# Loading the first input pair in two-chunk transfers, in an FFT-then-SoLU kernel on Trainium2

## The chip, the cores and the metric

The kernel runs on one core of one Trainium2 chip. The metric is device time in microseconds (us) of one execution; below 0.2% (2.4 us) a difference can't be told from no change. Engines are called PE (TensorE, matmul), DVE (VectorE), ACT (ScalarE), POOL (GpSimd) and SP (SyncE, which only issues transfers here). POOL issues the indirect (gathering) transfers; these go through another queue (q0) than SP's (q1).

## What is computed

```python
# x: (8, 3136, 256) float32; w_in (256, 1024), w_out (1024, 256), g_ln (1024): float64
X = np.fft.fft(np.fft.fft(x, axis=1), axis=2).real      # (8, 3136, 256)
x = X.reshape(25088, 256)
h = x @ w_in
e = np.exp(h - h.max(-1, keepdims=True))
solu = h * e / (e.sum(-1, keepdims=True) + 1e-09)
ln = (solu - mean(solu)) / np.sqrt(var(solu) + 1e-06) * g_ln
out = ln @ w_out                                        # (25088, 256) float32
```

## The kernel before

The sequence length 3136 is split as 49 x 64 (`N1`, `N2`), and the batch of 8 into four pairs (`Pair`). One pair gives 98 partitions (`PR`: two batch entries by 49 rows n1); row n1 of an entry is 64 positions of 256 floats, so neighbouring partitions lie 64 KB apart in DRAM. Because the input is real, position n2 is folded with its mirror position: only 32 of 64 positions (`NH`) are transformed. They are worked in eight **chunks** (`NC`) of four positions (`CH`); a chunk is 4 KB in each partition, 392 KB in all.

For each chunk `load` (L107) issues two transfers: SP fetches `xa` (L115), POOL gathers the mirrored rows `xb` through an index table (L117). The last chunk also fetches `x0` (L123). `add_mirror` (L132) adds the two on DVE, `fold` (L140) folds the features into `y` on DVE, `transform1` (L151) multiplies `y` with the table `F` on PE (L182), ACT copies the result to a tile `z` (L185), and `keep` (L189) writes 20 or, for later pairs, all of its 100 rows to a DRAM buffer `zd`. When all eight chunks are in `zd`, `turn` (L192) reads it back turned round, and `transform2` (L200) makes the input of a unit of 128 tokens. The hundred units (four pairs by 25) then run through a software pipeline: `up` (L233, two products with `Wi`), `even`, `join`, exponent, product, square, transposition and `down` (products with `Wo`).

The first pair has nothing to hide behind, and its load shares the start with the weights. These are float64 and are turned to float32 on the chip: four pieces of `w_in` are loaded (`piece_in`, L480) into `raw_in`; each goes through `exponent_in` (DVE L483, three ACT instructions L505 to L507) and `narrow_in` (DVE L483, L519, L522, L527); `product_in` (L577) multiplies them with the DFT table `Q`. `w_out` is loaded to `raw_out` by `load_out` (L589) and narrowed after the last chunk.

The order on every engine is the order of the program text (`tc.manual_schedule()`). In the start this is, on SP: index table, pieces 0 and 1, x of chunk 0, `F`, piece 2, chunk 1, piece 3, chunks 2 and 3, `Q`, `g_ln`, chunks 4 and 5; then, between the chunks' work, chunk 6 (after the fold of chunk 0), the `zd` write of chunk 0, chunk 7 (after the fold of chunk 1) and so on. Chunks 2 to 5 go into spare tiles that the main loop needs later (the `uT` buffers, "rooms" of four 4 KB rows each: `xa` and `xb` of two chunks), the others into the two buffers of `xpool`. On DVE, the program order is: exponents 0 and 1, narrowing 0 and 1, exponent 2, chunk 0, narrowing 2, exponent 3, chunk 1, narrowing 3, chunks 2 to 7, exponents of `w_out`. `load_out` stands after the fold of chunk 3 in the text and so behind the `zd` write of chunk 2 on SP; `product_in(0)` follows the transform of chunk 3 on PE, `product_in(1)` and `(2)` that of chunk 7.

A transfer on SP has one of eight completion semaphores in turn, and waits until the transfer eight places before it has landed. A transfer of 98 partitions runs on 14 of the 16 DMA engines, seven rows on each: of the 16 counts of its semaphore, 14 come as its engines end, spread over some microseconds.

Of the kernel before, what the change touches and what calls it, by code (L numbers as in the profile page):

```python
# [9 lines left out]
FP32 = mybir.dt.float32  # L10
# [7 lines left out]
P = 128  # L18
# [5 lines left out]
PR = 2 * N1  # L24
ZR = 4 * NK
CH = 4
NC = NH // CH

KG = 5
# [6 lines left out]
def kernel(  # L36
# [19 lines left out]
    nc = tc.nc  # L56
    B, S, D = x.shape
    FF = moe_w_in.shape[1]
    KF = FF // P
# [5 lines left out]
    x_pn = x.rearrange("b (n1 n2) d -> (b n1) n2 d", n2=N2)  # L65
# [10 lines left out]
    fpool = ctx.enter_context(tc.tile_pool(name="fpool", bufs=2))  # L76
# [3 lines left out]
    F = const.tile([PR, 6, ZR], FP32, name="F")  # L80
# [4 lines left out]
    Ws = const.tile([P, 4, KF // 2, P], FP32, name="Ws")  # L85
# [9 lines left out]
    def result(i):  # L95

        return ps_m.tile([P, 2 * D], FP32, tag=f"m{i % 4}", name="ps_m")

    class Pair:
        def __init__(self, p):
            self.p = p
            self.raw, self.y, self.y0 = {}, {}, None
            self.g, self.zs, self.done = {}, {}, []

    def load(pr, c, room=None):  # L107

        r = slice(pr.p * PR, (pr.p + 1) * PR)
        if room is None:  # L110
            xa = xpool.tile([PR, CH, D], FP32, tag="xa", name="xa")
            xb = xpool.tile([PR, CH, D], FP32, tag="xb", name="xb")
        else:
            xa, xb = (t.rearrange("p (l d) -> p l d", d=D) for t in room)
        nc.sync.dma_start(out=xa, in_=x_pn[r, c * CH + 1 : (c + 1) * CH + 1, :])  # L115
        i = pr.p * NC + c
        nc.gpsimd.indirect_dma_start(  # L117
            out=xb.rearrange("p l d -> p (l d)"), out_offset=None, in_=x_g,
            in_offset=bass.IndirectOffsetOnAxis(ap=idx[0:PR, i : i + 1], axis=0))
        x0 = None  # L120
        if c == NC - 1:
            x0 = xpool.tile([PR, 1, D], FP32, tag="x0", name="x0", bufs=1)
            nc.sync.dma_start(out=x0, in_=x_pn[r, 0:1, :])  # L123
        pr.raw[c] = (xa, xb, x0)
# [7 lines left out]
    def add_mirror(pr, c, engine):  # L132

        xa, xb, _ = pr.raw[c]
        n = CH - 1 if c == NC - 1 else CH
        a, rb = xa[:, 0:n, :], xb[:, ::-1, :][:, 0:n, :]
        engine.tensor_tensor(out=a[:, :, 1:D], in0=a[:, :, 1:D], in1=rb[:, :, D - 1 : 0 : -1], op=ALU.add)
        engine.tensor_tensor(out=a[:, :, 0:1], in0=a[:, :, 0:1], in1=rb[:, :, 0:1], op=ALU.add)

    def fold(pr, c):  # L140

        xa, _, x0 = pr.raw.pop(c)
        y = xpool.tile([PR, CH, D], FP32, tag="y", name="y")
        copy = nc.scalar.copy if pr.p else nc.vector.tensor_copy
        fold_features(y, xa, copy)
        pr.y[c] = y
        if c == NC - 1:
            pr.y0 = xpool.tile([PR, 1, D], FP32, tag="y0", name="y0", bufs=1)
            fold_features(pr.y0, x0, copy)

    def transform1(pr, s):  # L151

        c, l = divmod(2 * s, CH)
        if s == 0:
            pr.zd = dram.tile([ZR, NH, D], FP32, tag="zd", name="zd")
        if l == 0:

            if pr.p or c < 2:  # L160
                pr.z = zpool.tile([ZR, CH, D], FP32, tag="z", name="z")
            elif c < 4:
                z = fpool.tile([P, FF], FP32, tag="u", name="z_u", bufs=2)
                pr.z = z[0:ZR].rearrange("p (l d) -> p l d", l=CH)
            elif c < 6:
                pr.z = Ws.rearrange("p (h w) c k -> h p (w c k)", h=2)[c - 4, 0:ZR].rearrange("p (l d) -> p l d", l=CH)
            elif c == 6:
                pr.z = spool.tile([ZR, CH, D], FP32, tag="z6", name="z6")
            else:
                pr.z = gpool.tile([P, KG, D], FP32, tag="g", name="z_g")[0:ZR, 0:CH, :]  # L170
            pr.zs[c] = pr.z
        y = pr.y[c]
        ps = result(0 if pr.p else s).rearrange("p (l d) -> p l d", l=2)
        if s == NH // 2 - 1:
            parts = [(ps[0:ZR, 0], y[:, l], 0), (ps[0:ZR, 1], pr.y0[:, 0], 1), (ps[0:ZR, 1], y[:, l + 1], 2)]
        else:
            parts = [(ps[0:ZR], y[:, l : l + 2], 0)]
        pr.done.append(s)
        first = True
        for o, i, t in parts:  # L180
            for h, cs in enumerate((EVEN, ODD)):
                nc.tensor.matmul(o[..., cs], F[:, 2 * t + h, :], i[..., cs], start=first, stop=True,  # L182
                                 skip_group_check=True)
                first = False
        nc.scalar.copy(pr.z[:, l : l + 2, :], ps[0:ZR])  # L185
        if l == CH - 2:
            keep(pr, c, slice(0, ZR if pr.p else 4 * KG))

    def keep(pr, c, rows):  # L189
        nc.sync.dma_start(out=pr.zd[rows, c * CH : (c + 1) * CH, :], in_=pr.zs[c][rows])  # L190
# [304 lines left out]
    def confine(unit, here=False):  # L495

        if unit is None:
            return
        if here:
            bits(unit, unit, -896.0, ALU.add, 0.0, ALU.max)  # L500
            bits(unit, unit, 255.0, ALU.min, 2.0 ** 23, ALU.mult)
            return

        u = unit.bitcast(FP32)
        nc.scalar.activation(out=u, in_=unit, func=ACT.Relu, bias=limits[:, 0:1])  # L505
        nc.scalar.activation(out=u, in_=u, func=ACT.Relu, bias=limits[:, 1:2], scale=-1.0)
        nc.scalar.activation(out=unit, in_=u, func=ACT.Identity, bias=limits[:, 2:3], scale=-(2.0 ** 23))  # L507
# [109 lines left out]
    def ahead(pr, i):  # L617

        if i == (pr.p - 1) * NK:
            load(pr, 0)  # L620
            load(pr, 1)
        for c in range(NC):
            if i == SUMS[pr.p][c]:
                add_mirror(pr, c, nc.gpsimd)
            if i == SUMS[pr.p][c] + 1:
                fold(pr, c)
                if c + 2 < NC:
                    load(pr, c + 2)

    def ahead_pe(pr, i, half):  # L630

        for c in range(NC):
            if i == SUMS[pr.p][c] + 3:
                transform1(pr, c * CH // 2 + half)
# [7 lines left out]
    with tc.manual_schedule():  # L642
        pairs = [Pair(p) for p in range(NP)]
        first, weights = pairs[0], Weights()
        nc.sync.dma_start(out=idx, in_=mirror)
        make_identity(nc, ident)

        rooms = {}
        for c in range(2, 6, 2):
            room = fpool.tile([P, 2, KF, 4, 64], FP32, tag="uT", name="room", bufs=2)  # L650
            room = room[0:PR].rearrange("p w c i m -> p (w c i m)").rearrange("p (a n) -> p a n", a=4)
            rooms[c], rooms[c + 1] = [room[:, i] for i in (0, 1)], [room[:, i] for i in (2, 3)]
        weights.load_in()
        for c in range(4):
            weights.piece_in(c)
            if c:
                load(first, c - 1, rooms.get(c - 1))
            if c == 1:
                nc.sync.dma_start(out=F, in_=f_tab)
        load(first, 3, rooms[3])  # L660
        weights.load_tables()
        for c in range(4, 6):
            load(first, c, rooms[c])
        nc.vector.memset(ones, 1.0)
        nc.vector.memset(neg_half, -0.5)
        bits(top_bit, neg_half[:, 0:1].bitcast(I32), 31, ALU.logical_shift_right, 31, ALU.logical_shift_left)
# [3 lines left out]
            nc.vector.memset(t, 0.0)  # L670
        weights.exponent_in(0)
        weights.exponent_in(1)
        for c in range(NC):

            if c == 0:
                weights.narrow_in(0)
                weights.narrow_in(1)
            elif c < 3:
                weights.narrow_in(c + 1)
            if c < 2:  # L680
                weights.exponent_in(c + 2)
            add_mirror(first, c, nc.vector)
            fold(first, c)
            if c == NC - 1:
                for i in range(3):
                    weights.exponent_out(i)
            if c + 6 < NC:
                load(first, c + 6)
            if c == 3:
                weights.place_out()  # L690
                for i in range(2):
                    weights.load_out(i)
                weights.load_table(0)
                weights.mid()
                weights.scale_out()
            for s in range(CH // 2):
                transform1(first, c * CH // 2 + s)
            if c == 3:
                weights.product_in(0)

        turn(first, 0, nc.sync, 0, 2)
# [14 lines left out]
            take2(t, transform2(pairs[0], t.k1))  # L716
            spread(t)
        confine(weights.units[-1])
        for c in (2, 3, 0, 1, 4, 5, 6, 7):
            keep(first, c, slice(4 * KG, ZR))  # L720
        weights.load_table(1)
        lag = 4
        whole = 4
# [241 lines left out]
```

## Time and profile before

| | |
|---|---|
| median of 5 runs | 1178.15 us (1176.97 to 1179.09) |
| profiled execution | 1179.41 us |
| its span, first to last instruction | 1177.5 us |
| PE busy | 1132.9 us, 96% |
| DVE busy | 1005.9 us, 85% |
| ACT busy | 762.2 us, 65% |
| POOL busy | 598.4 us, 51% |
| granted PE clock, mean | 0.997 |
| last fold of the first pair ends on DVE, and DVE goes on with `raw_out` | 48.05 us from the start |
| first `even` of the main pipeline (DVE L244) | 60.98 us |

The profiled execution is 1.26 us above the median of the runs. In the windows view a row gives, for a stretch of time, its length, the busy time of each engine with the number of instructions, the granted PE clock, the mean busy share of the 16 DMA engines, and the GB/s that they moved. In the timeline a row gives the start and length in us, engine, line, operation and tiles, and in brackets the idle time of the engine ahead of it with what ended it. SPq is SP's issue of a transfer, not the transfer.

### The profile page before, as it was taken

What the parts mean: (1) busy time and instruction counts of PE and PEld (TensorE: products, weight loads), DVE (VectorE), ACT (ScalarE), POOL (GpSimd) and SP (SyncE); (2) the same over time, 40 slices, a digit from 0 to 9 for tenths busy, and PEclk for the clock granted to TensorE, in tenths of its full rate; (3) what the DMA queues carried; (4) which work ended last, traced back from release to release, by engine and by line L of the source; (5) the groups of instructions that cost most, each with busy time, mean ns of one, the idle gap of its engine ahead of it and who ended that gap; (6) DMA issues with size and microseconds to landing.
All of it is one profiled execution on the core that took longest, in us unless ns stands there. A gap on an engine that the chain in (4) does not pass through costs nothing. (4 is left out here: it accounts for less than half of the span.)

```text
span 1177.5 us, 18577 instructions
## 1 busy us (share of the span) xinstructions
PE 1132.9 (96%) x5850; PEld 881.8 (75%) x5850; DVE 1005.9 (85%) x1376; ACT 762.2 (65%) x1841; POOL 598.4 (51%) x558
## 2 busy tenths in 40 slices
PE   1989999999999999999999999999999999999997
PEld 1556787877877777878777777778777787778786
DVE  6889999998878999999879999999887888888860
ACT  3577766767656767667656666676666676667651
POOL 3036666563565566563556666554544334433444
PEclk9999999999999999999999999999999999999999
DMA  9772998865987988865879899865775565745553
GB/s 232 203 189 63 178 180 181 177 144 129 176 178 173 183 168 183 180 142 133 176 148 188 173 183 185 174 147 134 153 152 138 136 151 126 154 108 138 127 120 104
DMA packets 458466, 185.55 MB, mean 158 GB/s; under 512 B 425751, under 2 KB 440351, under 8 KB 458369
## 3 DMA queue, kind: packets, MB, share of 16 engines
q1 hardware_dynamic: 444608, 146.22, 60.2%
q0 software_dynamic: 13760, 38.16, 12.5%
q8 instruction: 47, 0.77, 0.3%
q14 instruction: 51, 0.41, 0.1%
HBM read 44.78 MB, written 38.80 MB: 71 GB/s over the span
## 5 line engine op out<-in xcount | busy, mean ns | idle before, releaser
L443 PE MATMUL ps_m<-Wo,uT 128*128 128x256 f32 x1632 | 370.7, 381 | 2.9 <-ACT uT L321 2.0
L238 PE MATMUL ps_h<-Wi,q 128*128 128x512 f32 x800 | 360.7, 593 | 1.6 <-DVE nmax L252 1.6
L443 PEld LDWEIGHTS ps_m<-Wo,uT 128*128 128x128 f32 x1632 | 315.2, 197 | 34.1 <-ACT uT L321 2.2
L268 DVE SCALAR_TENSOR_TENSOR u<-h,u 128x1024 f32<-128x1024 f32 x196 | 266.0, 1365 | 50.8 <-ACT u L261 46.8
L238 PEld LDWEIGHTS ps_h<-Wi,q 128*128 128x128 f32 x800 | 145.9, 190 | 148.1 <-issue 140.0
L275 ACT ACTIVATE h<-u,usum 128x1024 f32<-128x1024 f32 x196 | 224.4, 1145 | 33.8 <-DVE u L268 33.8
L354 POOL TENSOR_TENSOR S<-uT 128x512 f32<-128x512 f32 x94 | 130.2, 1386 | 208.8 <-issue 138.6
L261 ACT ACTIVATE u<-h,neg 128x1024 f32<-128x1024 f32 x196 | 225.4, 1150 | 6.4
L304 DVE STREAM_TRANSPOSE v<-u 128x1024 f32<-128x1024 f32 x192 | 228.0, 1226 | 0.1
L291 POOL TENSOR_TENSOR rs<-v,neg_half 128x2 f32<-128x2 f32 (+1 forms) x100 | 72.5, 725 | 249.6 <-ACT v L284 249.5
L252 DVE CUSTOM_DVE_ANT_0 h<-ev,ps_h 128x1024 f32<-128x1024 f32 x100 | 122.2, 1222 | 33.3 <-PE ps_h L238 23.7
L244 DVE SCALAR_TENSOR_TENSOR ev<-w_mid,r,ps_h 128x1024 f32<-128x1024 f32 x100 | 126.8, 1268 | 24.1 <-PE ps_h L238 20.6
L359 PE MATMUL ps_m<-Ws,S 128*128 128x128 f32 x1128 | 141.5, 275 | 1.0 <-ACT ot L390 1.0
L216 ACT COPY q<-ps_m 128x256 f32<-128x256 f32 x100 | 36.8, 368 | 161.7 <-PE ps_m L210 158.1
L359 PEld LDWEIGHTS ps_m<-Ws,S 128*128 128x128 f32 x1128 | 133.6, 192 | 1.7 <-issue 1.6
L252 DVE CUSTOM_DVE_ANT_0 h<-h,ps_h 128x1024 f32<-128x1024 f32 x96 | 117.3, 1221 | 13.8
L454 POOL DMA_INDIRECT out_dram<-ot,idx x96 | 100.7, 1049 | 31.6 <-issue 19.2
L359 PE MATMUL ps_m<-Wo,uT 128*128 128x128 f32 x752 | 104.2, 282 | 0.1
L182 PE MATMUL ps_m<-y,F 98*100 98x258 f32 (+3 forms) x288 | 72.6, 388 | 28.1 <-DVE y L130 26.1
L210 PEld LDWEIGHTS ps_m<-T,g 128*128 128x128 f32 x400 | 60.1, 191 | 50.2 <-issue 40.1
L359 PEld LDWEIGHTS ps_m<-Wo,uT 128*128 128x128 f32 x752 | 96.1, 196 | 0.9 <-issue 0.5
L259 ACT ACTIVATE neg<-nmax 128x1 f32<-128x1 f32 x196 | 38.4, 196 | 79.5 <-DVE nmax L252 79.4
(87 smaller groups left out, 1186.4 us busy)
## 6 DMA issues: line engine op xcount, KB each, us to landing
uT<-v SPq DMA_DIRECT2D x752, 128.0 KB
out_dram<-ot SPq DMA_DIRECT2D x100, 128.0 KB
g<-zd POOLq DMA_DIRECT2D x72, 160.0 KB, 5.5
xa<-in_x_dram SPq DMA_DIRECT2D x28, 392.0 KB
zd<-z SPq DMA_DIRECT2D x24, 400.0 KB
raw_in<-in_moe_w_in_dram SPq DMA_DIRECT2D x4, 512.0 KB
raw_out<-in_moe_w_out_dram SPq DMA_DIRECT2D x2, 1024.0 KB
r<-q SPq DMA_DIRECT2D x100, 0.5 KB
```

The source lines that it names most:

```text
L182: nc.tensor.matmul(o[..., cs], F[:, 2 * t + h, :], i[..., cs], start=first, stop=True, skip_group_check=True)
L238: nc.tensor.matmul(ps[:, fs], t.q[:, c * P : (c + 1) * P], Wi[:, c, fs], start=True, stop=True)
L244: nc.vector.scalar_tensor_tensor(out=t.ev, in0=w_mid, scalar=t.r, in1=ps, op0=ALU.mult, op1=ALU.add)
L252: nc.vector.tensor_tensor_reduce(out=t.h[s], in0=t.h[0] if s else t.ev, in1=t.odd, scale=1.0 if s else -0.5, scalar=-3.0e38, op0=ALU.add, ...
L261: nc.scalar.activation(out=t.u[s], in_=t.h[s], func=ACT.Exp, bias=t.neg[:, s : s + 1], accum_out=t.esum[:, s : s + 1])
L268: nc.vector.scalar_tensor_tensor(out=t.u[s], in0=t.h[s], scalar=1.0, in1=t.u[s], op0=ALU.mult, op1=ALU.mult, accum_out=t.usum[:, s : s + 1])
L275: nc.scalar.activation(out=t.h[s], in_=t.u[s], func=ACT.Square, bias=t.usum[:, s : s + 1], scale=-float(FF), accum_out=t.ssq[:, s : s + 1])
L304: nc.vector.transpose(out=t.batch.v[:, t.w, :, o], in_=t.u[s])
L354: nc.gpsimd.tensor_tensor(out=t.S[:, j], in0=a, in1=b, op=op)
L359: nc.tensor.matmul(o, a[:, c], b[:, c], start=start and c == 0, stop=c == n - 1, skip_group_check=True)
L443: nc.tensor.matmul(ps, uT[:, c, :, s], Wo[:, c, :], start=(c == 0), stop=(c == KF - 1))
L454: dma = nc.gpsimd.indirect_dma_start(out=out, out_offset=bass.IndirectOffsetOnAxis(ap=idx[:, i : i + 1], axis=0), in_=t.ot[s], in_offset=None)
```

## The change

Processing order becomes 0, 4, 1, 5, 2, 6, 3, 7 (`ORDER`). Chunks c and c + 4, which lie 16 KB apart in a partition's row, are fetched for c = 0, 1, 2 by one transfer on SP (`load_two`), whose inner order is: a partition's 4 KB of chunk c, its 4 KB of chunk c + 4, the next partition. The mirrored rows are gathered as before, one indirect transfer for a chunk; chunks 3 and 7 are loaded singly into `xpool`. A third room is taken from the second buffer of the `v` tile, so that no load of the first pair waits for a fold: all are issued ahead of the chunks' work. SP's order is now: index table, pieces 0 and 1, chunks 0 + 4, `F`, pieces 2 and 3, chunks 1 + 5, `Q`, `g_ln`, chunks 2 + 6, chunk 3, chunk 7. The tiles for `z` and the PSUM buffers are handed out by place in the new order.

```diff
+    ORDER = (0, 4, 1, 5, 2, 6, 3, 7)
...
+    def load_two(pr, c, room):
+        r = slice(pr.p * PR, (pr.p + 1) * PR)
+        both = x_pn[r, c * CH + 1 : (c + NC) * CH + 1, :].rearrange("p (a n) d -> p a (n d)", a=2)
+        nc.sync.dma_start(out=room[:, 0:2], in_=both[:, :, 0 : CH * D])
+        for a in range(2):
+            load(pr, c + 4 * a, (room[:, a], room[:, 2 + a]))
+
     def load(pr, c, room=None):
...
             xb = xpool.tile([PR, CH, D], FP32, tag="xb", name="xb")
+            nc.sync.dma_start(out=xa, in_=x_pn[r, c * CH + 1 : (c + 1) * CH + 1, :])
         else:
             xa, xb = (t.rearrange("p (l d) -> p l d", d=D) for t in room)
-        nc.sync.dma_start(out=xa, in_=x_pn[r, c * CH + 1 : (c + 1) * CH + 1, :])
...
-        for c in range(4):
-            weights.piece_in(c)
-            if c:
-                load(first, c - 1, rooms.get(c - 1))
-            if c == 1:
-                nc.sync.dma_start(out=F, in_=f_tab)
-        load(first, 3, rooms[3])
+        for tag in ("uT", "uT", "v"):
+            shape = [P, 2, KF, 4, 64] if tag == "uT" else [P, 2, FF, 2]
+            room = fpool.tile(shape, FP32, tag=tag, name="room", bufs=2)
...
+            rooms.append(room.rearrange("p (a n) -> p a n", a=4))
+        for c in range(2):
+            weights.piece_in(c)
+        load_two(first, 0, rooms[0])
+        nc.sync.dma_start(out=F, in_=f_tab)
+        for c in range(2, 4):
+            weights.piece_in(c)
+        load_two(first, 1, rooms[1])
         weights.load_tables()
-        for c in range(4, 6):
-            load(first, c, rooms[c])
+        load_two(first, 2, rooms[2])
+        for c in (3, 7):
+            load(first, c)
...
-        for c in range(NC):
-            if c == 0:
+        for i, c in enumerate(ORDER):
+            if i == 0:
                 weights.narrow_in(0)
                 weights.narrow_in(1)
-            elif c < 3:
-                weights.narrow_in(c + 1)
-            if c < 2:
-                weights.exponent_in(c + 2)
+            elif i < 3:
+                weights.narrow_in(i + 1)
+            if i < 2:
+                weights.exponent_in(i + 2)
             add_mirror(first, c, nc.vector)
             fold(first, c)
...
-            if c + 6 < NC:
-                load(first, c + 6)
-            if c == 3:
+            if i == 3:
                 weights.place_out()
...
-        for c in (2, 3, 0, 1, 4, 5, 6, 7):
-            keep(first, c, slice(4 * KG, ZR))
+        for i in (2, 3, 0, 1, 4, 5, 6, 7):
+            keep(first, ORDER[i], slice(4 * KG, ZR))
```

More of the change, by code (lines that the diff above doesn't have):

```diff
@@ L158, in transform1 @@
         if l == 0:
-            if pr.p or c < 2:
+            i = ORDER.index(c)
+            if pr.p or i < 2:
                 pr.z = zpool.tile([ZR, CH, D], FP32, tag="z", name="z")
-            elif c < 4:
+            elif i < 4:
                 z = fpool.tile([P, FF], FP32, tag="u", name="z_u", bufs=2)
                 pr.z = z[0:ZR].rearrange("p (l d) -> p l d", l=CH)
-            elif c < 6:
-                pr.z = Ws.rearrange("p (h w) c k -> h p (w c k)", h=2)[c - 4, 0:ZR].rearrange("p (l d) -> p l d", l=CH)
-            elif c == 6:
+            elif i < 6:
+                pr.z = Ws.rearrange("p (h w) c k -> h p (w c k)", h=2)[i - 4, 0:ZR].rearrange("p (l d) -> p l d", l=CH)
+            elif i == 6:
                 pr.z = spool.tile([ZR, CH, D], FP32, tag="z6", name="z6")
@@ L172, in transform1 @@
         y = pr.y[c]
-        ps = result(0 if pr.p else s).rearrange("p (l d) -> p l d", l=2)
+        ps = result(0 if pr.p else 2 * ORDER.index(c) + s % 2).rearrange("p (l d) -> p l d", l=2)
         if s == NH // 2 - 1:
@@ L646 @@
         make_identity(nc, ident)
[L648 to L652, printed above, removed]
-        weights.load_in()
-        for c in range(4):
-            weights.piece_in(c)
-            if c:
-                load(first, c - 1, rooms.get(c - 1))
-            if c == 1:
-                nc.sync.dma_start(out=F, in_=f_tab)
-        load(first, 3, rooms[3])
+        weights.load_in()
+        rooms = []
+        for tag in ("uT", "uT", "v"):
+            shape = [P, 2, KF, 4, 64] if tag == "uT" else [P, 2, FF, 2]
+            room = fpool.tile(shape, FP32, tag=tag, name="room", bufs=2)
+            room = room[0:PR].rearrange("p w c i m -> p (w c i m)" if tag == "uT" else "p a f b -> p (a f b)")
+            rooms.append(room.rearrange("p (a n) -> p a n", a=4))
+        for c in range(2):
+            weights.piece_in(c)
+        load_two(first, 0, rooms[0])
[3 more added lines that the diff above has]
+        load_two(first, 1, rooms[1])
         weights.load_tables()
-        for c in range(4, 6):
-            load(first, c, rooms[c])
+        load_two(first, 2, rooms[2])
+        for c in (3, 7):
+            load(first, c)
         nc.vector.memset(ones, 1.0)
@@ L672 @@
         weights.exponent_in(1)
-        for c in range(NC):
-            if c == 0:
+        for i, c in enumerate(ORDER):
+            if i == 0:
                 weights.narrow_in(0)
                 weights.narrow_in(1)
-            elif c < 3:
-                weights.narrow_in(c + 1)
-            if c < 2:
-                weights.exponent_in(c + 2)
+            elif i < 3:
+                weights.narrow_in(i + 1)
+            if i < 2:
+                weights.exponent_in(i + 2)
             add_mirror(first, c, nc.vector)
             fold(first, c)
-            if c == NC - 1:
-                for i in range(3):
-                    weights.exponent_out(i)
-            if c + 6 < NC:
-                load(first, c + 6)
-            if c == 3:
+            if i == NC - 1:
+                for j in range(3):
+                    weights.exponent_out(j)
+            if i == 3:
                 weights.place_out()
-                for i in range(2):
-                    weights.load_out(i)
+                for j in range(2):
+                    weights.load_out(j)
                 weights.load_table(0)
@@ L697 @@
                 transform1(first, c * CH // 2 + s)
-            if c == 3:
+            if i == 3:
                 weights.product_in(0)
```

## The prediction

> **What bounds the start now.** The page shows PE at 96% of the whole span, so over the long run only the moment at which the main pipeline starts can move the end; the change touches nothing behind it. I therefore read the windows of the first 50 us, then DVE's waits and timeline there, then PE's.
>
> ```profile
> core 0: us, PE busy (x) PEld busy (x) DVE busy (x) ACT busy (x) POOL busy (x), PEclk, DMA share, GB/s
> 5.00:10.00 5.00, 0.00 (x0) 0.00 (x0) 2.66 (x6) 3.71 (x6) 3.78 (x5) 1.00 1.00 290
> 10.00:20.00 10.00, 0.33 (x1) 0.33 (x2) 6.41 (x13) 2.68 (x4) 1.86 (x2) 1.00 1.04 260
> 20.00:30.00 10.00, 5.27 (x13) 3.14 (x13) 6.90 (x13) 3.34 (x5) 1.18 (x1) 1.00 0.96 212
> 30.00:40.00 10.00, 8.66 (x25) 5.42 (x24) 8.33 (x17) 4.09 (x9) 0.00 (x0) 1.00 0.94 225
> 105.00:105.50 0.50, 0.50 (x6) 0.50 (x6) 0.50 (x1) 0.00 (x0) 0.50 (x1) 1.00 1.05 360
> ```
>
> From 5 to 40 us the DMA engines are full (share 0.94 to 1.04), yet move only 212 to 290 GB/s. The last row is a later chunk of x (pair 1, chunk 2) whose 98 rows of the same 64 KB pitch go alone on SP's queue: 360 GB/s. So the start is bound by DMA, and its packets are slow.
>
> ```profile
> 16.52 0.43 DVE L483 TENSOR_SCALAR scratch<-raw_in 128x512 int32<-128x512 int32 x1 [3.49 <-DMA raw_in<-in_moe_w_in_dram]
> ...
> 24.99 0.43 DVE L483 TENSOR_SCALAR scratch<-raw_in 128x512 int32<-128x512 int32 x1 [3.00 <-DMA raw_in<-in_moe_w_in_dram]
> ...
> 37.24 1.22 DVE L137 TENSOR_TENSOR room<-room 98x1020 f32<-98x1020 f32 x1 [1.59 <-DMA room<-in_x_dram]
> ...
> 48.05 0.76 DVE L483 TENSOR_SCALAR scratch<-raw_out 128x512 int32<-128x512 int32 x2
> ```
>
> DVE waits three times: for piece 2 of `w_in`, for piece 3, and at 37.24 for chunk 4. From there four chunks run back to back, 10.81 us to 48.05.
>
> ```profile
> 47.82 2.39 PE L182 MATMUL ps_m<-y,F 98*100 98x258 f32 x16 [0.39 <-DVE y L130]
> 50.05 3.60 PE L577 MATMUL wps<-w_in,Q 128*128 128x512 f32 x8
> 53.48 3.60 PE L577 MATMUL wps<-w_in,w_mid 128*128 128x512 f32 x8
> 56.92 0.61 PE L210 MATMUL ps_m<-T,g 128*128 128x128 f32 x4
> 58.46 0.71 PE L210 MATMUL ps_m<-T,g 128*128 128x128 f32 x4 [0.93 <-ACT q L216]
> ```
>
> PE waits for DVE's last folds, then runs on with 0.93 us of idle through `product_in` to the first units; the first `even` follows at 60.98. So the path is: landing of the chunk that DVE waits for, four chunks on DVE, PE, main pipeline.
>
> **Landings before**, from the trace's record of each semaphore's last count (us): piece 1 7.68, chunk 0 9.64, F 12.60, piece 2 16.50, chunk 1 20.25, piece 3 24.96, chunk 2 28.86, chunk 3 31.61, chunk 4 37.15, chunk 5 38.95, chunk 6 40.04, chunk 7 42.28. The mirrored rows land ahead of them: chunks 0 to 5 at 12.77, 15.86, 19.36, 23.40, 27.02, 30.46.
>
> **The change, part by part.**
> *Bytes and queues.* The same rows are fetched. q0 was never empty from 7.5 to 30 us although chunk 6's gather waited for a fold (POOL issued it at 18.45): by 30 us 676 of its 784 rows had been moved, the four of chunks 6 and 7 not all. Two gathers issued earlier (POOL's row: 1.18 us each, on an engine idle there) only lengthen a queue. On SP, two x transfers are issued at 27.55 and 28.92 while room transfers are still to land until 38.95; issuing them earlier buys nothing, and three issues fewer at 0.3 to 0.5 us each lie beside a full queue: 0. As the queue is served in order, a transfer now lands when as many bytes lie ahead of it as before.
>
> *Order.* Pair 0 + 4 stands ahead of `F` and piece 2. Piece 2 has one x chunk more ahead of it; that is worth 3.75 us (chunk 1's own 16.50 to 20.25), so it lands at 20.25. Piece 3 has the same bytes ahead as before: 24.96. Pair 1 + 5 ends where chunk 3 ended: 31.61. Pair 2 + 6 ends where chunk 5 ended: 38.95. Chunks 3 and 7 come where 6 and 7 did: 40.04 and 42.28. The pair has one semaphore, so its first chunk waits for its second.
>
> *DVE, by its own durations.* Exponent 2, first chunk and narrowing 2 took 16.52 to 21.99, 5.47; from 20.27 they end at 25.74, behind piece 3, whose wait is gone. Exponent 3, second chunk and narrowing 3 took 24.99 to 30.37, 5.38: 31.12. Third chunk: 31.61 plus 0.09 from landing to start (37.15 to 37.24), 31.70; two chunks at 2.60 (37.24 to 39.85, 39.85 to 42.45) end at 36.90. Fifth chunk waits for pair 2 + 6: 39.04. Four chunks: 49.85. Before 48.05: **1.80 us later**. The 7.2 us that DVE now idles ahead of 20.27 cost nothing by themselves, since the DMA wait at 39.04 ends last, 2.14 us behind DVE.
>
> *Behind it.* `w_out`: its issue follows SP's `zd` write of the third chunk, 4.96 us after that chunk's fold (33.06 to 38.02): 34.30 + 4.96 = 39.26, while x still lands until 42.28, so it has the same bytes ahead and lands near its old 49.51; DVE's old wait of 0.73 us for it falls away. That shortens only DVE's own line (then +1.07), which had 1.73 us of idle ahead of the first `even`; PE's line carries the whole 1.80, as do the `zd` write of the last chunk (landed at 52.66) and `turn`. Rooms cost nothing: room 0 is free after the second chunk, ahead of its reuse by `raw_out`; the `v` buffer is wanted only from unit 4 on. Behind the start DVE is busy 9.68 and 9.63 of 10 us in 80 to 100, so no slack swallows the shift.
>
> *Packet time, the unknown.* Between 7.5 and 37.5 us a 4 KB packet took 268 ns on q0 and 276 on q1 in the mean (median 259); alone, 163 at 105 us. Is the surplus an address conflict that rows 16 KB apart relieve? Against it: the lone chunk with 14 engines in step at a 64 KB pitch runs at 163; and while q1 moved F and piece 2, which have no such pitch, beside q0 (10 to 12.5 us), both queues already showed 249 and 252. Slowness thus goes with both queues at work, which the change leaves. For it: the best 2.5 us window (15 to 17.5) has 242, the worst (20 to 22.5) 313 and 298, so something in the addresses may matter. Bounds: 163 below, 305 above; I take 272, unchanged, nearest in kind.
>
> The Trainium skill ("DMA: Bandwidth & Descriptors", "Latency and other measured facts") has a row on HBM row pitch: copies at pitches of 512 KiB and more lose rate, and a few KiB of offset restore it. By it the change would bring the packets toward the lone rate, the first rival below; the row at 105 us shows no loss at 64 KB, and I follow the row.
>
> **The rivals.**
> 1. *Faster packets.* Landings after 7.68 shrink by a factor f. At 220 ns, midway between 272 and about 165, f = 0.81: piece 2 at 17.9, pair 2 + 6 at 7.68 + 31.27 x 0.81 = 33.0. Then DVE binds from piece 2 on: 17.9 + 0.02 + 5.47 + 5.38 + 5.20 + 10.81 = 44.8, 3.3 us earlier: **1174.9**. At 242 ns f = 0.89: pair 2 + 6 at 35.5, end at 46.4, 1.65 earlier. At 163 f = 0.60, end at 42.1, 6.0 earlier: 1172.2. For: the spread of the windows. Against: the two rows above. It beats the order's loss once pair 2 + 6 lands ahead of 37.15, f below 0.94.
> 2. *Slower packets.* With all sixteen transfers under way and q1 touching two places in turn, the start runs as the window of 20 to 25 does, 303 ns, f = 1.115: pair 2 + 6 lands at 42.5, four chunks end at 53.4, 5.4 later: **1183.5**. For: that window. Against: q0 and q1 were both full before. It shows beyond the forecast from a landing after 39.5.
> 3. *The shift is swallowed:* DVE's line, not PE's, sets the start (+1.07 or less), and part is lost in the main pipeline's waits: about 0.5 us, **1178.7**. For: the lost 0.73 wait. Against: PE's unbroken line from 47.82.
> That the change does not do what it says: a transfer could pass a partition's two rows as one packet of 8 KB, giving q1 a larger share. The packets of `raw_out` are 2 KB, its DRAM run, though 8 KB lie together in SBUF, so I expect 4 KB; it would act like rival 1.
>
> **How the numbers follow.** Profiled execution 1179.41 + 1.80 = 1181.2; it stands 1.26 above the median, so the median goes to 1178.15 + 1.80 = 1180.0. Chances: forecast 0.44 (own range 1178.4 to 1181.5, the slowest engine of a transfer varying by 1 to 1.5 us), rival 1 0.28, rival 2 0.18, rival 3 0.10. Range for 8 in 10: 1174.5 to 1183.0, with about half of rival 1's spread and half of rival 2's cut off. Below 1175.8 (0.2%, what a measurement can tell from no change): 0.23, all of rival 1. Above 1180.5: 0.17 of the forecast and 0.18 of rival 2, 0.35. Between: 0.42.
>
> **What would show it.** In the profile after: DVE's wait for piece 2 ends near 20.3 instead of 16.52; no wait for piece 3; a wait near 31.7 and one of about 2 us ending near 39.0 for a room; `raw_out` exponents begin near 49.9 without their wait; first `even` near 62.8; GB/s from 10 to 40 us as before. If GB/s there are well above 212 to 260, rival 1 has come; if below, rival 2. If the `raw_out` exponents move and the first `even` does not, rival 3.

## The result

The changed kernel takes 1180.52 us in the median against 1178.16, a ratio of 1.0021 with a 95% interval of [1.0015, 1.0027]: 2.36 us slower (the interval is 1.8 to 3.2 us). The forecast was 1180.0, from a shift of 1.80 us, which lies at the lower edge of that interval. The two profiled executions hide the difference: 1179.29 after, 1179.41 before. The one of before stands 1.25 us above its median, the one of after 1.23 below.

Windows of the changed kernel, with the columns as before:

```profile
5.00:10.00 5.00, 0.00 (x0) 0.00 (x0) 3.35 (x7) 4.03 (x6) 3.78 (x5) 1.00 1.03 307
10.00:20.00 10.00, 0.00 (x0) 0.00 (x0) 5.07 (x9) 2.36 (x4) 3.12 (x3) 1.00 1.04 258
20.00:30.00 10.00, 7.46 (x16) 4.28 (x16) 9.08 (x18) 4.41 (x7) 0.00 (x0) 1.00 0.99 233
30.00:40.00 10.00, 8.32 (x23) 5.23 (x24) 6.45 (x14) 2.92 (x7) 0.00 (x0) 1.00 0.94 240
```

The DMA engines are as full as before and move 233 to 258 GB/s from 10 to 40 us, where before had 212 to 260. Neither faster nor slower packets have come. DVE's timeline and waits:

```profile
17.24 0.43 DVE L495 TENSOR_SCALAR scratch<-raw_in 128x512 int32<-128x512 int32 x1 [4.87 <-DMA raw_in<-in_moe_w_in_dram]
...
28.84 1.22 DVE L148 TENSOR_TENSOR room<-room 98x1020 f32<-98x1020 f32 x1 [0.58 <-DMA room<-in_x_dram]
...
37.61 1.22 DVE L148 TENSOR_TENSOR room<-room 98x1020 f32<-98x1020 f32 x1 [3.48 <-DMA room<-in_x_dram]
...
48.20 1.09 DVE L495 TENSOR_SCALAR scratch<-raw_out 128x512 int32<-128x512 int32 x3
...
61.14 1.28 DVE L256 SCALAR_TENSOR_TENSOR ev<-w_mid,r,ps_h 128x1024 f32<-128x1024 f32 x1 [2.58 <-ACT scratch L518]
```

The pattern is the forecast one. The wait for piece 2 has grown from 3.49 to 4.87 us, that for piece 3 is gone, the fifth chunk waits 3.48 us for pair 2 + 6 (1.59 for chunk 4 before), and the wait for `w_out` is gone. DVE's idle ahead of the first `even` has grown from 1.73 to 2.58: its own line comes earlier there, and PE's does not:

```profile
47.97 2.39 PE L194 MATMUL ps_m<-y,F 98*100 98x258 f32 x16 [0.39 <-DVE y L141]
50.20 3.60 PE L589 MATMUL wps<-w_in,Q 128*128 128x512 f32 x8
53.64 3.60 PE L589 MATMUL wps<-w_in,w_mid 128*128 128x512 f32 x8
57.07 0.61 PE L222 MATMUL ps_m<-T,g 128*128 128x128 f32 x4
```

PE still waits for DVE's last fold and then runs on, each row 0.15 us later than before, as is the last fold (48.20 against 48.05). One profile of each kernel can't show the median's 2.36 us; further profiles were needed of both.

### The profile page after: what moved, and what is told of

Its sections match the earlier page's. It is cut to its first block, busy times and chain, and to the rows that moved or that the text cites. A ratio compares the mean times of both kernels' runs of the same rounds, so it can differ in the third digit from the quotient of the medians.

```text
span 1177.5 us, 18567 instructions
## 1 busy us (share of the span) xinstructions
PE 1133.4 (96%) x5850; PEld 881.9 (75%) x5850; DVE 1005.3 (85%) x1376; ACT 761.8 (65%) x1841; POOL 598.4 (51%) x558
## 5 line engine op out<-in xcount | busy, mean ns | idle before, releaser
L264 DVE CUSTOM_DVE_ANT_0 h<-ev,ps_h 128x1024 f32<-128x1024 f32 x100 | 122.2, 1222 | 34.0 <-PE ps_h L250 23.5
```

Of the source, the lines that this page charges most:

```text
L264: nc.vector.tensor_tensor_reduce(out=t.h[s], in0=t.h[0] if s else t.ev, in1=t.odd, scale=1.0 if s else -0.5, scalar=-3.0e38, op0=ALU.add, ...
```

## The experiments

Theory: the place of a chunk's last byte in SP's queue sets when DVE may go on, and a pair places its first chunk behind its second. Rivals: the addresses (16 KB apart, rows in turn) change the rate of the packets; the loss lies behind the start. Each group of kernels ran on one chip with runs of the kernel before between them; a ratio is always to that kernel.

**e1, the changed kernel again** (no edit).

> The changed kernel once more, for a second profile: its first one shows the last-chunk fold only 0.15 us later than before (48.20 against 48.05) and a time 1.2 us below its own median. Theory (the third pair's landing sets when the last four chunks run): the landing of pair 2 + 6 varies between executions and is usually later than the 37.5 us of that profile; this profile shows it anywhere from 37.5 to 40, the first even always 23.5 to 24 us behind it, and the time follows one for one; ratio to before 1.002. Rival (the loss lies behind the start, in the main pipeline): the first even again near 61.1 and the time again near 1180.5.

Measured: 1180.20, ratio 1.0017 [1.0004, 1.003]. DVE in its profile:

```profile
36.91 1.22 DVE L148 TENSOR_TENSOR room<-room 98x1020 f32<-98x1020 f32 x1 [2.07 <-DMA room<-in_x_dram]
...
60.53 1.28 DVE L256 SCALAR_TENSOR_TENSOR ev<-w_mid,r,ps_h 128x1024 f32<-128x1024 f32 x1 [2.58 <-ACT scratch L518]
...
78.67 1.28 DVE L256 SCALAR_TENSOR_TENSOR ev<-w_mid,r,ps_h 128x1024 f32<-128x1024 f32 x1 [1.88 <-DMA r<-q]
```

Pair 2 + 6 landed still earlier (36.82, ahead of the expected 37.5 to 40), and yet this execution took 1180.63. The landing did not carry over to the time one for one; with the first `even` at 60.53 this is near the sign given for the rival, a loss behind the start. 1.88 us went to a place that neither theory nor forecast had, unit 2's `r`. That transfer of 0.5 KB stands behind the `zd` writes and the table `T` in SP's queue and landed at 78.56.

**e9, the kernel before again** (no edit).

> The kernel before, unchanged, as a kernel of its own: a further profile of it and a measure of what two equal kernels differ by. Theory: its fifth chunk lands between 35.4 and 37.2, the first even comes 23.5 us behind it at 59 to 61, and its time is that even plus 1118 to 1119; ratio 0.999 to 1.001.

Measured: 1177.60, ratio 1.0004 [0.9995, 1.0013].

```profile
34.95 1.22 DVE L137 TENSOR_TENSOR room<-room 98x1020 f32<-98x1020 f32 x1 [2.92 <-DMA room<-in_x_dram]
...
58.48 1.28 DVE L244 SCALAR_TENSOR_TENSOR ev<-w_mid,r,ps_h 128x1024 f32<-128x1024 f32 x1 [2.06 <-ACT scratch L506]
...
74.70 1.28 DVE L244 SCALAR_TENSOR_TENSOR ev<-w_mid,r,ps_h 128x1024 f32<-128x1024 f32 x1
```

The same kernel, chunk 4 started 2.29 us earlier than in the profile that the forecast was made from. Its landing, 34.85, lies outside the range expected (35.4 to 37.2), and so does its first `even` (58.48 for 59 to 61); the 23.5 us between the two held (23.63).

**e5 and e6, the table behind `r`**, in the changed kernel and in the one before:

```diff
-        weights.load_table(1)
         lag = 4
...
             if i == 0:
+                weights.load_table(1)
                 turn(first, 1, nc.sync)
```

> The changed kernel with the second half of the twiddle table (T, 640 KB, wanted from unit 5 on) issued behind the two r transfers of units 2 and 3 instead of ahead of them. In one profile of the changed kernel the third even waited 1.88 us for r, which lay behind T and the z writes in SP's queue. If the loss sits there (rival), this kernel comes down to the time of before, 1177.5 to 1178.5, and the same edit leaves the kernel before as it is. If it sits in the landing of the x pairs (theory), both kernels gain alike, at most 1 us, and stay 1.5 to 2.5 us apart. In the profile the third even waits for no r: third even minus first even 16.1 to 16.2 us.

> The kernel before with the same edit. Theory: at most 1 us faster than before (its profile shows r landing 0.4 us ahead of the third even, so only some executions wait). Rival: unchanged, within 0.3 us.

Measured: e5 1180.56, ratio 1.0019 [1.0005, 1.0032]; e6 1178.35, ratio 1.0000 [0.9987, 1.0014]. No `r` wait in either profile (third `even` 16.16 and 16.17 us behind the first), but no gain either; the two stay 2.2 us apart. So the rival of e5, that the loss sits at `r`, fails: the changed kernel did not come down to the time of before. For e6 the interval is too wide to tell the small gain from none. The edit does not touch the start, so both give one more profile of it.

Six profiles together, in us. The time less the third `even` is 1101.6 to 1102.3 in all six: whatever differs has happened by then.

| kernel | fifth chunk starts on DVE | first `even` | third less first `even` | that execution's time |
|---|---|---|---|---|
| before | 37.24 | 60.98 | 16.18 | 1179.41 |
| before, e9 | 34.95 | 58.48 | 16.22 | 1176.38 |
| before, table late, e6 | 35.51 | 59.04 | 16.17 | 1177.04 |
| mean | 35.90 | 59.50 | 16.19 | 1177.61 |
| changed | 37.61 | 61.14 | 16.17 | 1179.29 |
| changed, e1 | 36.91 | 60.53 | 18.14 | 1180.63 |
| changed, table late, e5 | 37.69 | 61.53 | 16.16 | 1179.28 |
| mean | 37.40 | 61.07 | 16.82 | 1179.73 |

The fifth chunk starts 1.50 us later, the first `even` 1.57 later, and 0.63 comes from the one execution with the `r` wait: together 2.20, where the mean times differ by 2.12. With three executions of each the split is an estimate: the three starts of before alone lie 2.29 us apart.

**e2, pairs split into two transfers:**

```diff
-        both = x_pn[r, c * CH + 1 : (c + NC) * CH + 1, :].rearrange("p (a n) d -> p a (n d)", a=2)
-        nc.sync.dma_start(out=room[:, 0:2], in_=both[:, :, 0 : CH * D])
+        for a in range(2):
+            c1 = c + 4 * a
+            nc.sync.dma_start(out=room[:, a], in_=x_pn[r, c1 * CH + 1 : (c1 + 1) * CH + 1, :].rearrange("p l d -> p (l d)"))
```

> The changed kernel with each pair fetched by two single transfers, one behind the other, so that each chunk has its own landing; order, rooms and early issue stay. Theory: the fifth chunk is released one chunk earlier, some 1.8 us (37.2 instead of 38.95 in the reckoning), the sixth never waits; 1178.2 to 1178.8, ratio to before 1.000 to 1.0005. Rival (alternating the rows of two places speeds or slows the queue itself): the mean GB/s from 10 to 40 us changes by over 5% and the time by over 2 us against the changed kernel in the direction of the packets.

Measured: 1178.09, ratio 1.0003 [0.9992, 1.0015], 2.11 us under e1 on the same chip.

```profile
36.12 1.22 DVE L149 TENSOR_TENSOR room<-room 98x1020 f32<-98x1020 f32 x1 [2.00 <-DMA room<-in_x_dram]
...
60.08 1.28 DVE L257 SCALAR_TENSOR_TENSOR ev<-w_mid,r,ps_h 128x1024 f32<-128x1024 f32 x1 [2.57 <-ACT scratch L519]
```

The third `even` comes 16.17 us behind the first; GB/s from 10 to 40 us are 241, as in the changed kernel (244, 248, 241). Order, rooms and early issue are still those of the change, so those cost nothing that shows; joining two chunks in one transfer is what is left. The intervals of e1 and e2 overlap, but drawing again and again from the twelve runs of each puts the difference between their medians at 1.0 to 3.2 us. The landings show the mechanism: here the fifth chunk landed at 36.02 and the sixth at 37.60, and the joined pair lands where the sixth does (37.52, 36.82 and 37.60 in the changed kernel's three profiles). So joining would have cost the fifth chunk 1.58 us in this execution.

**e4, single chunks in the middle:**

```diff
-    ORDER = (0, 4, 1, 5, 2, 6, 3, 7)
+    ORDER = (0, 4, 1, 5, 3, 7, 2, 6)
...
-        load_two(first, 2, rooms[2])
         for c in (3, 7):
             load(first, c)
+        load_two(first, 2, rooms[2])
```

> The changed kernel with the two single chunks 3 and 7 fetched ahead of pair 2 + 6 and worked as fifth to eighth chunk in the order 3, 7, 2, 6. Same transfers, same bytes. Theory: the fifth chunk is again released when five chunks are in (37.2), and the pair, last in the queue near 42, is wanted only at 42.4: 1178.2 to 1178.9, ratio 1.000 to 1.0006. Rival (the loss is in the pair transfers or in early issue as such): unchanged, near 1180.5.

Measured: 1179.49, ratio 1.0017 [1.0006, 1.0027]; the theory's number was wrong, and by the time alone the kernel can't be told from the changed one, as its rival had it. DVE's waits, then PE, in the one profile there is:

```profile
30.58 1.22 DVE L148 TENSOR_TENSOR room<-room 98x1020 f32<-98x1020 f32 x1 [1.29 <-DMA room<-in_x_dram]
...
36.08 1.22 DVE L148 TENSOR_TENSOR xa<-xa,xb 98x1020 f32<-98x1020 f32 x1 [0.21 <-DMA xa<-in_x_dram]
...
45.13 0.69 DVE L139 TENSOR_TENSOR y<-room 98x508 f32<-98x508 f32 x1 [2.13 <-PE ps_m L194]
```

```profile
33.42 6.51 PE L194 MATMUL ps_m<-y,F 98*100 98x258 f32 x16 [3.09 <-DVE y L141]
39.77 3.60 PE L589 MATMUL wps<-w_in,Q 128*128 128x512 f32 x8
43.20 5.80 PE L194 MATMUL ps_m<-y,F 98*100 98x258 f32 x32
```

The fifth chunk no longer waits (0.21), as the theory had it. But pair 1 + 5 releases the third chunk only at 30.58; PE idles 3.09 us until 33.42, and with `product_in(0)` between the transforms it is then the bound: DVE waits 2.13 us for one of the two `y` buffers. In this execution the second pair costs as the third did, through PE instead of DVE.

**e10, pairs 8 KB apart, and e3, neighbours.** e10 takes (0, 2), (1, 3), (4, 6), then 5 and 7; e3 takes (0, 1), (2, 3), (4, 5), then 6 and 7. The core of e10:

```diff
-    ORDER = (0, 4, 1, 5, 2, 6, 3, 7)
+    ORDER = (0, 2, 1, 3, 4, 6, 5, 7)
...
-        both = x_pn[r, c * CH + 1 : (c + NC) * CH + 1, :].rearrange("p (a n) d -> p a (n d)", a=2)
+        both = x_pn[r, c * CH + 1 : (c + 4) * CH + 1, :].rearrange("p (a n) d -> p a (n d)", a=2)
```

> The changed kernel with pairs 8 KB apart (0 + 2, 1 + 3, 4 + 6, then 5 and 7 singly), the rows of both in turn as in the change, still pieces of 4 KB. Theory (place in the queue, not distance): as the changed kernel, 1179.5 to 1181, ratio 1.0012 to 1.0025, third pair landing 36.8 to 38, GB/s from 10 to 40 us 238 to 250. Rival (16 KB is what counts): GB/s and landing differ from the changed kernel's by over 5%.

> The changed kernel with pairs of neighbouring chunks (0 + 1, 2 + 3, 4 + 5, then 6 and 7 singly), so that the two rows of a partition lie 4 KB apart instead of 16 KB; everything else as in the change. Theory (place in the queue, not address): the same loss, 1180.0 to 1181.0, ratio 1.0015 to 1.0025. Rival (addresses): if 16 KB apart relieves a conflict this is slower than the changed kernel by 1 to 5 us, with fewer GB/s from 10 to 40 us; if it makes one, faster by as much.

Measured: e10 1180.12, ratio 1.0020 [1.0009, 1.0031], GB/s 250, third pair landed at 36.85; its profile again has an `r` wait, of 1.70 us. Half the distance changes nothing that shows. e3 1179.13, ratio 1.0013 [1.0003, 1.0022], under the 1180.0 to 1181.0 expected, and it can't answer its question: neighbours make one run of 8 KB in DRAM, and the trace shows their packets as 8 KB. In taking turns SP's queue then moves 8 KB for POOL's 4 (57 packets against 66 from 20 to 23 us). GB/s from 10 to 40 us are 262 and the third pair lands at 35.31, so the fifth chunk starts at 35.40, not later than in the kernel before (35.90 in the mean). Still the median is slower than before. The landing does not explain that; the profile, of an execution 1.3 us under the kernel's median, shows only a wait of 0.85 us for PE's `y`. It stays open.

**e7, no gather.** On e2, the first pair's mirrored rows go as plain transfers on SP, in straight order:

```diff
+        if pr.p:
             nc.gpsimd.indirect_dma_start(
...
+        else:
+            nc.sync.dma_start(out=xb, in_=x_pn[r, (15 - c) * CH : (16 - c) * CH, :])
```

**e8, all x on POOL**, on e2: the straight rows too are issued with `nc.gpsimd.dma_start`. **e11** moves the load of `g_ln` behind that of `idx` in e8; **e12** adds the late table of e5 to e11.

> The kernel of the split pairs, but the mirrored rows of the first pair are fetched by SP as plain transfers of the mirror chunk's rows, in straight and not mirrored order of n1; so the mirror sum of the first pair is left out of the computation. Same bytes, same 4 KB pieces at 64 KB pitch, nothing on POOL's queue. If the slow packets come from two queues at work (theory), the 4 KB packets fall from 240 to 300 ns to 160 to 210, GB/s from 10 to 30 us rise from some 245 to over 310, and the last x lands before 35 us. If they come from the addresses (rival), GB/s stay between 220 and 270 and the last x lands near 40.

> The kernel of the split pairs with the straight rows of the first pair issued by POOL too, so that all x is on POOL's queue and SP's has only weights and tables. If two queues at work are the cause, the queues compete only until the weights are in, near 20 us; then POOL's runs alone near 200 ns a packet and the fifth chunk lands near 31 instead of 36 to 37; the folds end 2 to 4 us earlier and the time falls to 1174 to 1176.5. If it is the addresses, nothing but the order of landing changes: 1177 to 1179.5.

> The kernel with all x of the first pair on POOL's queue, and g_ln (1,024 pieces of 4 B) loaded right behind the index table instead of behind Q. In the profile of e8 those pieces took turns with POOL's 4 KB packets and landed at 37.84, with x0 at 40.30 and w_out at 48.35 behind them; DVE waited 2.42 us for w_out. Theory: w_out lands ahead of 46 and that wait goes; but PE's line sets the first even, so at most 1 us is gained on e8: 1174.5 to 1176.5, ratio 0.997 to 0.9985. Rival (DVE's line sets it): 2 us or more, under 1174.

> The kernel of e11 (all x of the first pair on POOL's queue, g_ln first) with T's second half behind the two r transfers, as in e5. The profile of e11 had its first even at 58.12 and its third waiting 1.14 us for r. Theory (both the landing of x and the wait for r count in the time): no wait for r, third even minus first 16.1 to 16.2; 1 us off e11's time, 1176.3 to 1177.2 beside a kernel before at 1177.8, ratio 0.998 to 0.9995, so a little faster than both kernels. Rival (what is won ahead of the first even is lost behind it): ratio 1.000 or above.

Measured: e7 one run of 1174.18; e8 1176.07, ratio 0.9987 [0.9971, 1.0003]; e11 1177.87, ratio 1.0005 [0.9996, 1.0014]; e12 1177.70, ratio 1.0000 [0.9991, 1.001]. Windows of e7 (all x on SP's queue) and of e11 (all x on POOL's; SP's has next to nothing there):

```profile
24.00:34.00 10.00, 8.29 (x20) 5.24 (x20) 9.61 (x17) 3.72 (x9) 0.00 (x0) 1.00 0.90 291
```

```profile
27.00:35.00 8.00, 6.29 (x17) 3.94 (x16) 7.85 (x15) 2.63 (x6) 1.20 (x1) 1.00 0.94 233
```

Rows of 4 KB at the same pitch: 291 GB/s on SP's queue at 0.90 of the engines, 233 on POOL's at 0.94. Expected was that the slow packets belong to two queues at work; e11's window, with one queue, says no. Nor are they a fixed rate of POOL's queue. In the kernel before, a gather of pair 1 has that queue to itself from 106 to 107 us; and in e11 itself the last chunks go faster:

```profile
106.00:107.00 1.00, 1.00 (x11) 1.00 (x10) 1.00 (x1) 0.97 (x2) 1.00 (x1) 1.00 0.89 291
```

```profile
35.00:37.00 2.00, 2.00 (x8) 1.13 (x7) 1.97 (x5) 1.35 (x4) 0.00 (x0) 1.00 0.90 283
```

Both are near what SP's queue reached in e7. And SP's queue too is slower in the start, 291 GB/s, than with the lone chunk of the prediction's row at 105 us, 360. So each queue has lost about a fifth in these windows against a lone transfer, with no second queue to share with. What costs it stays open.

In e7 the last x landed at 34.55 instead of near 40, the 4 KB packets took 206 ns in the mean (7.5 to 30 us; 267 to 268 on POOL's queue before), and the first `even` came at 57.26. From 10 to 30 us it moved 288 GB/s, above the range given for the rival and short of the 310 of the theory. It leaves the mirroring out, so it is a measure and no way out. In e8 the fifth chunk started at 30.78, near the 31 expected, but POOL's packets stayed at 285 ns in the mean from 19 to 34 us, where near 200 was expected. e8 looked faster but its interval takes in 1; e11 and e12 did not confirm it. In e11 `w_out` landed at 46.55 (expected ahead of 46), the wait for it fell to 0.64, the third `even` waited 1.14 for `r`, and the time missed the 1174.5 to 1176.5 expected; e12 lost the `r` wait, but its first `even` came at 61.41 where e11 had 58.12, and its ratio is the rival's, 1.000 or above. No version beats the kernel before beyond its interval.

## Why the prediction was right, and where its steps were off

*The size and its cause.* The step that carried the sum, pair 2 + 6 landing one chunk's place later and 1.80 us with it, measures 1.50 us at the fifth chunk and 1.57 at the first `even`, over three profiles of each. The term itself, from chunk 4's landing to chunk 5's in the kernel before, is 1.80 us in the profile that the forecast used, but 1.43 in e9 and 1.57 in e6, and 1.58 in e2. So the step is right and its size was somewhat high, while the median moved by more than the step. That the number came so near is partly luck: some 0.8 us of the 2.36 are not accounted for by it. That the shift passes whole is right: DVE's `raw_out` exponents start 1.56 us later in the mean (48.13 against 46.57), the first `even` 1.57, and the time less the third `even` is the same in all six within 0.7 us. The third rival, a shift swallowed behind the start, fails on that. The first two, faster or slower packets, fail on GB/s: 232, 254 and 247 from 10 to 40 us in the three profiles of before, 244, 248 and 241 in the changed kernel's. By e10, halving the distance has no effect that shows.

*What the sum left out.* (a) The wait for unit 2's `r`, 1.88 and 1.70 us in e1 and e10 and none in the changed kernel's first profile; neither of the two profiles of before with the table in its old place has it, though `r` landed only 0.1 us ahead of the third `even` in one of them (e9), as in the changed kernel's first. It may bring the rest up to 2.36 us. That is not shown: without it (e5) the ratio stayed at 1.0019. (b) PE as a second bound behind the second pair (e4): the forecast followed DVE alone from 31.70 to 36.90. PE was at work in its last term too: the four chunks that it calls back to back, 10.81 us, hold 0.23 us of waiting for `y`; without that they take 10.59 (e9).

*Absolute landings.* Piece 2 was forecast at 20.25 and landed at 17.22, 18.22 and 19.48; the fifth chunk was to start at 39.04 and did at 37.61, 36.91 and 37.69; the third was to wait until 31.70 and started at 28.84, 29.56 and 30.44, the last without a wait. All were too late; the one execution that they were built on was slow: chunk 4 started at 37.24 there and at 34.95 and 35.51 in others. The difference of two such sums came within 0.3 us of the measured 1.50, the sums did not; with three profiles of each kernel an agreement that close is also luck. One landing was misread, without weight in the sum: chunk 7's last count stands at 41.72, and the one at 42.28 comes after SP had issued the next transfer on that semaphore (41.79).

*The packet time.* "Slowness goes with both queues at work" was the failed step of the reasoning, though it did not touch the sum: e11 has slow packets with POOL's queue alone (233 GB/s), and in e7 SP's queue alone stays under the rate of the lone chunk (291 for 360). What makes them slow is open. The value taken (unchanged) held, and the distance between alternate rows did not change it.

*The row on HBM row pitch.* The row of the Trainium skill ("DMA: Bandwidth & Descriptors", "Latency and other measured facts") is about rows 512 KiB to 8 MiB apart, and restores the rate by adding 4 KiB to the pitch. The change leaves the pitch at 64 KB, so the row does not say what the prediction drew from it for rival 1. Here 16 KB or 8 KB between alternate rows changed no rate (241 to 250 GB/s, against 232 to 254 before).

*Early issue.* The change was hardly a test of it on SP. SP's issue of pair 2 + 6 lasted 19.1 us (chunk 4's lasted 14.3 before), so the last two x transfers were issued at 26.15 and 27.17 instead of 27.55 and 28.92. The last two gathers were issued 7.4 and 14.1 us earlier, and that brought nothing that shows.

## What to carry to other kernels

Where a start is bound by a queue that is full, joining two loads delays the first to the second's landing: split transfers at the granularity at which the next engine waits. Issuing gathers earlier into such a queue gave nothing here. Price the change by places in the queue ahead of the one wait that ends last, and look for the next bound (here PE, by its `y` buffers) before moving a wait. Take absolute landing times from several executions: one profile of each kernel showed no difference here, where the medians lie 2.36 us apart.

## What was not expected of the hardware

In the start POOL's queue alone moved 4 KB rows at 233 GB/s (e11, 27 to 35 us) and SP's alone at 291 (e7); a lone gather on POOL's reached 291, a lone load on SP's 360. The Trainium skill ("DMA: Bandwidth & Descriptors", "Issuing engine by pattern") calls transfers issued from SP generally faster; these runs agree in both pairs, though POOL's were gathers, or gathers and plain loads in turn, and SP's plain loads. Two rows that are neighbours in DRAM and in SBUF went as packets of 8 KB (e3), though the two halves belong to different chunks. And two executions of one kernel differ by 2.3 us at the fifth chunk (37.24 and 34.95), nearly the whole effect that was studied.
